# An FNet mixer gated with a SwiGLU block on one core: the opening loads, the first operand splits and the place of TensorE's flag read

## The chip, the core and the metric

The kernel runs on one core of a Trainium2 chip. A core has five engines that run their own instruction queues: TensorE (PE, matrix products, with its weight loads shown apart as PEld), VectorE (DVE), ScalarE (ACT), GpSimd (POOL) and SyncE (SP, which here only issues DMAs). The metric is the device time of one execution in microseconds (us). The kernel before took 355.21 us, the median of three runs (354.94 to 356.22).

## What is computed

The input `x` is 2048 x 512 in float32. Branch A is the real part of a two-dimensional Fourier transform, written with given cosine and sine matrices. Branch B is a SwiGLU block with 1376 hidden columns. A gate per row mixes the two:

```
g = sigmoid((x * gate_w).sum(-1, keepdims=True))
a = x @ dft_hid_re.T ; b = x @ dft_hid_im.T
A = dft_seq_re @ a - dft_seq_im @ b
B = (silu(x @ w1) * (x @ w3)) @ w2
out = g * A + (1 - g) * B
```

## The kernel before, in words

All products are of float32 values. Each operand is split into a rounded high part (a type that TensorE reads fast) and the low rest, and a product is three matmuls, high x high, high x low and low x high (`mm3`, line 131). The high part is a copy on ScalarE (`high`, line 114) or, for half of a tile, on VectorE (`high_by_both`, line 463, whose VectorE half is line 465); the low part is a subtraction on VectorE that reads the high part (`low`, line 117). Weights and `x` are cut into blocks and combined so that seven block products do the work of eight; these are the tiles `X`, `Y` and `Z`. The first group of them, written out by hand, accumulates in four banks `C`.

The program has three stretches. Up to about 207 us it forms the gate and up products of branch B (tiles `C`, `X`, `Y`, `Z`), 16 matmul groups of 128 x 512 per weight block, while VectorE and ScalarE split the next operands and sum products. Then come 528 matmuls of the down product (tile `H`). The end, from 321 us on, is the Fourier branch (tiles `O`, `E`, `Y`, `Yodd`) with the output stores. The Fourier branch uses symmetries of the cosine and sine matrices. That they hold is tested while the kernel runs; one value, the flag, says whether they do (lines 581 to 593). Every engine loads it into a register (lines 1328, 1342 and 1373) and then branches: with the symmetries there, the branch leaves out a general path (line 1380).

The order of instructions is the order of the Python code, engine by engine; nothing is rescheduled. The opening stands in lines 413 to 534. The array `first` packs, for each of 128 partitions, the first weight block and the blocks `B11` and `B21` of `x`: columns 0 to 255 are the first quarter of the weights (`W0[0]`), 256 to 1279 are `B11` in two halves of 512, 1280 to 1535 are another quarter, and so on to 3071. SyncE loads it in four pieces of 768 columns (lines 416 and 417), then two more blocks of `x` (`xs_B`, line 174) and the weight blocks 1 to 5 (`ws`, line 198). While the first piece is on its way, TensorE runs nine matmuls on constants (line 423, tile `wps`). Then lines 474 to 486 split the pieces as they come; the splits land in `xo` (`x`), `wa` (weights) and `a` (the quarter at 1280), and `half` (line 435) issues six matmuls each. For the first one the order of operands is: high weights x high `x`, high weights x low `x`, low weights x high `x`, for the first half of `x`, then high x high, low x high, high x low for the second.

After the opening, VectorE's queue holds without a pause: the splits of `B12` and `B22` (lines 490 to 493), the block differences (line 181), the splits of the next weight blocks and, from line 364 on, the sums of each item (`gate_up`). TensorE meets the results of that queue by semaphores.

Of the kernel before, what the change touches and what calls it, by code (L numbers as in the profile page):

```python
# [18 lines left out]
NTB = S // TB  # L19
NC = (F + P - 1) // P  # L20
NP2 = (NC + 1) // 2
WARM = 9
LOOK = 3
K = 9
TOL = 2.0 ** 40
# [5 lines left out]
def fnet_swiglu_gate_kernel(  # L31
# [27 lines left out]
    nc = tc.nc  # L59
# [26 lines left out]
    def bank(k, name):  # L86
        return psum.tile([P, 512], F32, tag=f"ps{k}", name=name)
# [20 lines left out]
    def free(*tiles):  # L108
        for t in tiles:
            _, places, at = HELD.pop(id(t))  # L110
            if places is not F4 or at not in GONE:
                places.append(at)

    def high(hi, src):
        nc.scalar.activation(hi, src, AF.Copy)  # L115

    def low(hi, lo, src):
        nc.vector.tensor_sub(lo, src, hi.bitcast(F32))  # L118

    def split(hi, lo, src):  # L120
        high(hi, src)
        low(hi, lo, src)
# [20 lines left out]
    def flat(ap):  # L143
        return ap.rearrange("p a n -> p (a n)")
# [268 lines left out]
    ctx.enter_context(tc.manual_schedule())  # L413
    XO[0] = xo0.tile([P, 2, 7, 2, 512], F32R, tag="xo", name="xo0")
    raw = xo1.tile([P, 2, 6, 2, 512], F32, tag="xo", name="raw")[:, 0].rearrange("p i q n -> p (i q n)")
    for n in range(4):
        nc.sync.dma_start(raw[:, 768 * n : 768 * n + 768], first[:, 768 * n : 768 * n + 768])
    ST[0, "B11"], ST[0, "B21"] = raw[:, 256:1280], raw[:, 1792:2816]
    W0 = [raw[:, at : at + 256] for at in (0, 1536, 2816, 1280)]
    warm = nc.const_aps.tensor(1.0, [P, 512], mybir.dt.bfloat16)  # L420
    wps = bank(7, "wps")
    for n in range(WARM):
        nc.tensor.matmul(wps, warm[:, :P], warm, start=True, stop=True)
# [11 lines left out]
    def half(i, j, w, x, start):  # L435

        wp = lambda h, sl: a21[:, h, sl] if w is None else WA[0][:, h, w, sl]
        xp = lambda q, h: b12[:, h, q * 512 : (q + 1) * 512] if x is None else XO[0][:, h, x, q, :]  # L440
        hh, lh, hl = (0, 0), (1, 0), (0, 1)
        order = [(r, *p) for r in range(2)
                 for p in ((hh, lh, hl) if x is None or r and w == x else (hh, hl, lh))]
        for n, (r, u, v) in enumerate(order):
            matmul(C[i, j], wp(u, slice(r * P, (r + 1) * P)), xp(r, v),
                   start=start and n == 0, stop=not start and n == 5)

    def xo_half(k, q):
        i = OPS.index(k)
        return XO[0][:, 0, i, q], XO[0][:, 1, i, q], ST[0, k][:, q * 512 : (q + 1) * 512]  # L450
# [12 lines left out]
    def high_by_both(hi, lo, src):  # L463
        high(hi[:, :256], src[:, :256])
        nc.vector.tensor_copy(hi[:, 256:], src[:, 256:])

    def split_by_both(hi, lo, src):
        high_by_both(hi, lo, src)
        low(hi, lo, src)

    def w0_parts(w):
        return flat(WA[0][:, 0, w : w + 1]), flat(WA[0][:, 1, w : w + 1]), W0[w]

    high_by_both(*xo_half("B11", 0))
    high(*w0_parts(0)[::2])
    low(*xo_half("B11", 0))
    low(*w0_parts(0))
    split(*xo_half("B11", 1))
    half(0, 0, 0, 0, True)
    split(a21[:, 0], a21[:, 1], W0[3])  # L480
    half(1, 0, None, 0, True)
# [91 lines left out]
    n = NI - 1 - LOOK  # L573
# [7 lines left out]
    def verdict():  # L581


        v = acc.rearrange("p (g n) -> p g n", n=16)
        nc.vector.scalar_tensor_tensor(v, v, TOL, rep_sum[:, :5, None].to_broadcast([P, 5, 16]),
                                       op0=ALU.mult, op1=ALU.is_le)
        nc.vector.tensor_reduce(flag[:, :1], acc, axis=mybir.AxisListType.X, op=ALU.add)

    def sum_flags(ps):
        nc.tensor.matmul(ps[:1, :1], flag[:, :1], nc.const_aps.tensor(1.0, [P, 1], F32), start=True, stop=True)  # L590

    def see_flags(ps):
        nc.vector.tensor_scalar(flag[:1, 2:3], ps[:1, :1], 80.0 * P, None, op0=ALU.is_lt)
# [40 lines left out]
    def work(eng, us, most=9, lag=None, over=0.3):  # L634


        NOW[0] += 1
        TOKENS[0] = min(TOKENS[0] + RATE[0], 1.5)
        lag = LAG[0] if lag is None else lag
        for i in ORDER[:LIMIT[0]]:  # L640
            of, cost, f, after, _, _, temps = QUEUE[i]
            if i in ISSUED or of != eng:
                continue
            if most == 0 or us < cost - over:
                break
            if i not in LOADED or NOW[0] - LOADED[i] < lag or temps and len(F4) < temps + RES[0]:
                continue
            if any(NOW[0] - ISSUED.get(k, NOW[0]) < (GAP.get(i, 1) if lag else 1) for k in after):
                continue
            HELD_BACK[0] -= temps  # L650
            f()
            ISSUED[i] = NOW[0]
            us -= cost
            most -= 1
        load_ahead(AHEAD[0])
        return us
# [561 lines left out]
    def next_two(name):  # L1218
        turn[0] += 1
        return psum.tile([P, 1024], F32, tag=f"two{(3, 1, 2, 0)[turn[0] % 4]}", name=name)  # L1220
# [76 lines left out]
    def of_d(im, odd):  # L1297
        at = 514 * im + 258 * odd
        return [DT[:, h, at : at + 258 - 2 * odd].rearrange("p (a n) -> p n a", a=2) for h in range(2)]

    def chain_two(to, terms):
        for n, (u, v) in enumerate(terms):
            for k, (i, j) in enumerate(((0, 0), (0, 1), (1, 0))):
                nc.tensor.matmul(to, u[i], v[j], start=n == k == 0, stop=n == len(terms) - 1 and k == 2,  # L1304
                                 skip_group_check=True)
# [3 lines left out]
    bad_in, seen = nc.alloc_registers("bad"), flag.bitcast(I32)[0:1, 2:3]  # L1309
    z_E = yp.tile([P, 2, 2, 516], F32R, tag="z_E2", name="z_E2")  # L1310

    def even(p):
        two = next_two(f"E2_{p}")
        ps = two[:, :258], two[:, 512:770]
        forms(*ps, ("E2",), range(2), p)
        z = Z["E2", p] = z_E[:, p]
        zh, zl = (z[:, h].rearrange("p (v n) -> p v n", v=2) for h in range(2))
        split(zh, zl, two.rearrange("p (v n) -> p v n", v=2)[:, :, :258])

    even(0)  # L1320
    for u, (kind, za, zb, n, swap) in enumerate(UNITS):
        if u == 4:
            even(1)
        ps = next_two(f"Y{u}")
        if u == 5:
            sum_flags(ps)
        if u == 8:
            nc.tensor.reg_load(bad_in[mybir.EngineType.PE], seen)

        def zs(p, at):  # L1330
            return [Z[kind, p][:, h, at : at + P] for h in range(2)]

        apart = u == len(UNITS) - 1
        po = next_two("Yodd") if apart else ps
        evens, odds = (v[:, lo:hi].rearrange("p (n a) -> p n a", a=2)
                       for v, lo, hi in ((ps, 254, 512), (po, 512, 768)))
        chain_two(evens, [(zs(0, za), of_d(0, 0)), (zs(1, zb), of_d(1, 0))])
        chain_two(odds, [(zs(1, za), of_d(0, 1)), (zs(0, zb), of_d(1, 1))])
        if u == 5:
            see_flags(ps)  # L1340
            for e in (nc.sync, nc.gpsimd, nc.scalar):
                e.reg_load(bad_in[e.engine], seen)
        r = yp.tile([P, 1024], F32, tag=f"r{u % 6}", name=f"r{u}")
        nb = NB.pop(u)

        def both(v):
            return v.rearrange("p (a m) -> p a m", a=2)[:, :, :256]

        for i in range(0 if apart else n):
            k = FIRST[u] + i  # L1350
            rv, nv = (both(v[:, i * D : i * D + D]) for v in (r, nb))
            src = both(ps[:, 255:769])[:, :, ::-1] if i ^ swap else both(ps[:, 254:770])
            nc.vector.scalar_tensor_tensor(rv, src, g_pos[:, k : k + 1], nv, op0=ALU.mult, op1=ALU.add)
        if apart:
            k = FIRST[u]
            for a, src in enumerate((ps[:, 255:511], po[:, 512:768])):
                at = slice(256 * a, 256 * a + 256)
                nc.vector.scalar_tensor_tensor(r[:, at], src[:, ::-1], g_pos[:, k : k + 1], nb[:, at],  # L1358
                                               op0=ALU.mult, op1=ALU.add)
                nc.sync.dma_start(out[k][:, at], r[:, at])  # L1360
            continue
        nc.sync.dma_start(out[FIRST[u] : FIRST[u] + n].rearrange("k p n -> p k n"),
                          r.rearrange("p (k n) -> p k n", k=2)[:, :n])
        if FIRST[u] > 7:
            free(nb)
        if u < 2:
            work("A", 3.6)
            work("D", 1.3)
        if u == 2:
            work_until(set(range(n_late)))  # L1370
        if u == 3:
            verdict()
    nc.vector.reg_load(bad_in[mybir.EngineType.DVE], seen)
    bad = nc.snap(bad_in, donate=True, min_val=0, max_val=0x3F800000)
    close(zo_a_cm, lp_cm)
# [255 lines left out]
```

## Time and profile before

| what | value |
|---|---|
| median of three runs | 355.21 us (354.94 to 356.22) |
| the profiled execution's own time | 355.75 us |
| its span, first to last instruction | 354.0 us |
| TensorE busy | 348.0 us, 98% of the span |
| VectorE, ScalarE, GpSimd busy | 311.2, 233.5, 73.3 us |
| moved by DMA | 103.03 MB, 291 GB/s in the mean |

A profile's times are counted from the first instruction of the span. A row of the timeline holds the start, the time from the first to the last of the merged instructions, the engine, the line of the kernel, the operation, output tile <- input tiles, shapes and the count; in brackets stands the idle time of that engine just before, and what ended it. Matmuls overlap, so six of them that start 0.216 us apart and take 0.379 us each stand as one row of 1.46 us.

### The profile page before, as it was taken

The numbers are of one execution on the slowest core, as the hardware profiler recorded it, in microseconds if no ns is written. First come the engines' busy times: TensorE is split into PE (matmuls) and PEld (weight loads), VectorE is DVE, ScalarE is ACT, GpSimd is POOL, SyncE is SP. The second block draws the span as 40 slices with busy tenths as digits, with TensorE's granted clock in tenths as the row PEclk, the third lists the DMA queues.
The fourth block names the chain that finished last, engine by engine and source line by source line (L and its number), as shares of the span: only waits on it lengthen the run. The fifth ranks groups of instructions, "written<-read, shape, count | busy, mean of one in ns | idle before, by whom it ended". The sixth has DMA issues, their size and how long they took to land.

```text
span 354.0 us, 5152 instructions
## 1 busy us (share of the span) xinstructions
PE 348.0 (98%) x1718; PEld 303.7 (86%) x1718; DVE 311.2 (88%) x442; ACT 233.5 (66%) x395; POOL 73.3 (21%) x121
## 2 busy tenths in 40 slices
PE   8999999999999999999999999999999999999994
PEld 4888888888888888888888888888888888889994
DVE  4999989999869788888887899989969989998983
ACT  5875866556648687775433399642588988879940
POOL 0012333323111132111113763335011002000000
PEclk9999999999999999999999999999999999999999
DMA  7669865669645779999999149997649999999276
GB/s 279 254 244 357 319 261 212 224 240 332 222 120 192 250 218 390 408 400 402 373 382 291 58 126 373 410 365 241 237 120 362 416 411 406 411 409 348 100 262 219
DMA packets 33952, 103.03 MB, mean 291 GB/s; under 512 B 5874, under 2 KB 6276, under 8 KB 33924
## 3 DMA queue, kind: packets, MB, share of 16 engines
q1 hardware_dynamic: 26340, 75.91, 58.2%
q0 software_dynamic: 7584, 26.77, 20.6%
q8 instruction: 14, 0.23, 0.3%
q14 instruction: 14, 0.11, 0.1%
HBM read 78.02 MB, written 24.65 MB: 290 GB/s over the span
## 4 chain that ended last, share of the span: by engine, by line
PE 96%; DMA 1%; ACT 1%; DVE 0%; issue 0%; SPq 0%; ACTq 0%
PE H L129 32%; PE X L129 30%; PE Z L129 15%; PE Y L129 8%; PE Y L1304 4%; PE C L129 3%; PE O L129 3%; PE E L129 1%; DMA raw<-first 1%; PE Yodd L1304 0%; DVE h L408 0%; ACT w2t L115 0%; ACT u L369 0%; DVE r L1358 0%; ACT xo L115 0%
## 5 line engine op out<-in xcount | busy, mean ns | idle before, releaser
L129 PE MATMUL H<-w2t,ht 128*128 128x512 f32 (+1 forms) x528 | 114.1, 379 | 0.0
L129 PEld LDWEIGHTS H<-w2t,ht 128*128 128x128 f32 (+1 forms) x528 | 99.8, 189 | 14.2
L129 PE MATMUL X<-xo,wb 128*128 128x512 f32 x378 | 88.6, 379 | 0.0
L129 PEld LDWEIGHTS X<-xo,wb 128*128 128x128 f32 x378 | 71.4, 189 | 10.2
L765 ACT ACTIVATE t<-t 128x1024 f32<-128x1024 f32 (+1 forms) x68 | 67.3, 992 | 1.5 <-DVE t L754 1.4
L320 POOL DMA_DIRECT2D hs<-h x36 | 19.6, 545 | 88.7 <-DVE h L391 63.5
L404 ACT ACTIVATE h<-X 128x512 f32<-128x512 f32 x21 | 12.5, 596 | 32.2 <-PE X L129 21.8
L129 PE MATMUL Z<-xo,wa 128*128 128x512 f32 x126 | 30.7, 380 | 0.0
L129 PE MATMUL X<-xo,wa 128*128 128x512 f32 x126 | 30.8, 380 | 0.0
L115 ACT ACTIVATE ht<-hr 128x1024 fp32r<-128x1024 f32 x19 | 20.0, 1053 | 16.3 <-PE H L129 10.6
L129 PE MATMUL Y<-xo,wa 128*128 128x512 f32 x126 | 30.6, 379 | 0.0
L129 PE MATMUL Z<-xo,wb 128*128 128x512 f32 x126 | 30.6, 379 | 0.0
L381 DVE TENSOR_TENSOR u<-u,X 128x512 f32<-128x512 f32 x21 | 14.4, 686 | 17.9 <-PE X L129 13.4
L129 PEld LDWEIGHTS Z<-xo,wa 128*128 128x128 f32 x126 | 23.7, 189 | 3.8 <-ACT u L369 0.4
L129 PEld LDWEIGHTS X<-xo,wa 128*128 128x128 f32 x126 | 23.7, 189 | 3.6 <-DVE wa L118 0.3
L129 PEld LDWEIGHTS Y<-xo,wa 128*128 128x128 f32 x126 | 23.8, 189 | 3.4
L129 PEld LDWEIGHTS Z<-xo,wb 128*128 128x128 f32 x126 | 23.8, 189 | 3.4
L754 DVE TENSOR_TENSOR t<-t,rep 128x1024 f32<-128x1024 f32 x21 | 24.7, 1220 | 0.6 <-DMA t<-wt 0.6
L118 DVE TENSOR_TENSOR ht<-hr,ht 128x1024 fp32r<-128x1024 f32 x19 | 23.1, 1217 | 0.0
L115 ACT ACTIVATE wa<-ws 128x768 fp32r<-128x768 f32 x19 | 15.9, 838 | 6.2 <-PE Z L129 5.9
L752 DVE TENSOR_TENSOR t<-t,rep 128x512 f32<-128x512 f32 x30 | 19.0, 684 | 0.0
L756 DVE TENSOR_TENSOR t<-t,rep 128x1024 f32<-128x1024 f32 x16 | 18.7, 1220 | 0.0
(210 smaller groups left out, 519.6 us busy)
## 6 DMA issues: line engine op xcount, KB each, us to landing
t<-wt SPq DMA_DIRECT2D x60, 512.0 KB, 9.3
hr<-hs SPq DMA_DIRECT2D x19, 512.0 KB, 8.8
hs<-h POOLq DMA_DIRECT2D x36, 256.0 KB, 4.4
wbsp<-wb POOLq DMA_DIRECT2D x16, 512.0 KB, 4.8
wb<-wbsp SPq DMA_DIRECT2D x16, 512.0 KB, 9.4
xr<-xw SPq DMA_DIRECT2D x8, 512.0 KB, 11.6
xs_B<-xt SPq DMA_DIRECT2D x6, 512.0 KB, 6.5
ws<-w POOLq DMA_DIRECT2D x6, 512.0 KB, 4.0
```

What stands on the lines that cost most here:

```text
L115: nc.scalar.activation(hi, src, AF.Copy)
L118: nc.vector.tensor_sub(lo, src, hi.bitcast(F32))
L129: nc.tensor.matmul(ps.rearrange("p (n a) -> p n a", a=2), u, turns(v)[:, some], **kw)
L320: nc.gpsimd.dma_start(hs[c][:, b * TB : (b + 1) * TB], h)
L381: nc.vector.tensor_add(u4, u4, x)
L404: nc.scalar.activation(g1, x, AF.Silu)
L752: f(*(v[:, 512 * a : 512 * a + 512] for v in (t, t, r)))
L754: nc.vector.tensor_sub(t, t, r)
L756: nc.vector.tensor_add(t, t, r)
L765: nc.scalar.activation(t[:, :n], t[:, :n], AF.Abs, accum_out=acc[:, i : i + 1])
L1304: nc.tensor.matmul(to, u[i], v[j], start=n == k == 0, stop=n == len(terms) - 1 and k == 2, skip_group_check=True)
```

## The change

It has three parts. First, `WARM` goes from 9 to 8, so one matmul on constants fewer runs at the start. Second, the array `first` is loaded in five pieces: columns 0 to 255 by GpSimd, then 256 to 767 (the first half of `B11`), 768 to 1535, 1536 to 2303 and 2304 to 3071 by SyncE. The splits behind it change order: the weights' high and low parts come first, then the first half of `B11`, with its high part done by both engines as before, and the second half of `B11` is now split by both engines too, where ScalarE copied its whole high part. Third, TensorE's load of the flag leaves its place ahead of the ninth unit of the Fourier branch and stands behind all its products, written twice.

```diff
-WARM = 9
+WARM = 8
...
-    for n in range(4):
-        nc.sync.dma_start(raw[:, 768 * n : 768 * n + 768], first[:, 768 * n : 768 * n + 768])
+    for n, (lo, hi) in enumerate(((0, 256), (256, 768), (768, 1536), (1536, 2304), (2304, 3072))):
+        (nc.sync if n else nc.gpsimd).dma_start(raw[:, lo:hi], first[:, lo:hi])
...
-    high_by_both(*xo_half("B11", 0))
-    high(*w0_parts(0)[::2])
-    low(*xo_half("B11", 0))
-    low(*w0_parts(0))
-    split(*xo_half("B11", 1))
+    split(*w0_parts(0))
+    split_by_both(*xo_half("B11", 0))
+    split_by_both(*xo_half("B11", 1))
...
-        if u == 8:
-            nc.tensor.reg_load(bad_in[mybir.EngineType.PE], seen)
...
+    for _ in range(2):
+        nc.tensor.reg_load(bad_in[mybir.EngineType.PE], seen)
     nc.vector.reg_load(bad_in[mybir.EngineType.DVE], seen)
```

This is VectorE's queue at the start of the program, as a difference: minus was there before, plus is there now. `wa` is the split of the first weights, `xo` that of `x`, `raw` the loaded array, `a` another quarter of the weights; `DMAHW0` is SyncE's first load, `DMASW0` GpSimd's.

```order
+L118 TENSOR_TENSOR wa_135<-raw,wa_135 128x256 [waits DMASW0_49,Activation_49]
 L465 CAST xo_100<-raw 128x256 [waits DMAHW0_49]
 L118 TENSOR_TENSOR xo_100<-raw,xo_100 128x512 [waits DVE_49,Activation_49]
-L118 TENSOR_TENSOR wa_135<-raw,wa_135 128x256 [waits Activation_49]
-L118 TENSOR_TENSOR xo_100<-raw,xo_100 128x512 [waits DMAHW1_49,Activation_49]
+L465 CAST xo_100<-raw 128x256 [waits DMAHW1_49]
+L118 TENSOR_TENSOR xo_100<-raw,xo_100 128x512 [waits DVE_49,Activation_49]
 L118 TENSOR_TENSOR a_128<-raw,a_128 128x256 [waits Activation_49]
 L465 CAST xo_100<-raw 128x256 [waits DMAHW2_49]
```

The weights' subtraction now stands at the head of VectorE's queue and waits for GpSimd's load and ScalarE's copy; a copy of a quarter of `B11` is new.

This is the end of TensorE's queue before; `Y` and `Yodd` are the last banks, `dt` and `z_E` operands of the Fourier branch, `tail` holds the flag.

```order
L1304 MATMUL Y_3326<-dt,z_E_3149 128x256 x6
L1328 TENSOR_LOAD tail [waits DVE_49]
L1304 MATMUL Y_3342<-dt,z_E_3149 128x258 [waits DVE_49,PE_49]
L1304 MATMUL Y_3342<-dt,z_E_3149 128x258 x5
L1304 MATMUL Y_3342<-dt,z_E_3149 128x256 x6
L1304 MATMUL Y_3359<-dt,z_E_3149 128x258 [waits DVE_49,PE_49]
L1304 MATMUL Y_3359<-dt,z_E_3149 128x258 x5
L1304 MATMUL Yodd<-dt,z_E_3149 128x256 [waits DVE_49]
L1304 MATMUL Yodd<-dt,z_E_3149 128x256 x5
L1380 COMPARE_AND_BRANCH
```

And this is the same end now (line numbers are those of the changed file, two lower).

```order
L1302 MATMUL Y_3343<-dt,z_E_3150 128x258 [waits DVE_49,PE_49]
L1302 MATMUL Y_3343<-dt,z_E_3150 128x258 x5
L1302 MATMUL Y_3343<-dt,z_E_3150 128x256 x6
L1302 MATMUL Y_3359<-dt,z_E_3150 128x258 [waits DVE_49,PE_49]
L1302 MATMUL Y_3359<-dt,z_E_3150 128x258 x5
L1302 MATMUL Yodd<-dt,z_E_3150 128x256 [waits DVE_49]
L1302 MATMUL Yodd<-dt,z_E_3150 128x256 x5
L1370 TENSOR_LOAD tail [waits DVE_49]
L1378 COMPARE_AND_BRANCH
```

The load stands behind the last product now, and it stands there once: of the two that are written, the built program keeps one, with the wait for VectorE ahead of it.

## The prediction, made before the changed kernel was run

> **What bounds the kernel now.** I read the page's shares first, then the chain that ended last.
>
> ```profile
> PE 348.0 (98%) x1718; PEld 303.7 (86%) x1718; DVE 311.2 (88%) x442; ACT 233.5 (66%) x395; POOL 73.3 (21%) x121
> PE 96%; DMA 1%; ACT 1%; DVE 0%; issue 0%; SPq 0%; ACTq 0%
> ```
>
> TensorE is busy 98% of the span and carries 96% of the chain, so only the waits left in its queue can be won. The view of waits, for its weight loads, names them.
>
> ```profile
> PEld C L129 <- ACT wa L115: 1.2, 1, 1.2
> PEld C L129 <- DVE xo L118: 0.5, 2, 0.3
> ...
> PEld X L129 <- DVE wa L118: 0.3, 1, 0.3
> ```
>
> The change touches the first two. Whether a gain there survives depends on the last row, a wait for VectorE. The timeline of the opening:
>
> ```profile
> 0.84 1.81 SPq L417 DMA_DIRECT2D raw<-first  x4
> 0.91 4.01 PE L423 MATMUL wps<-const-bfloat16-1.0 128*128 128x512 bf16 x9 [0.91 <-PEq L1618]
> ...
> 4.40 0.42 ACT L115 ACTIVATE xo<-raw 128x256 fp32r<-128x256 f32 x1 [2.16 <-DMA raw<-first]
> 4.40 0.29 DVE L465 CAST xo<-raw 128x256 fp32r<-128x256 f32 x1 [4.40 <-DMA raw<-first]
> 4.72 0.40 ACT L115 ACTIVATE wa<-raw 128x256 fp32r<-128x256 f32 x1
> 4.85 0.69 DVE L118 TENSOR_TENSOR xo<-raw,xo 128x512 fp32r<-128x512 f32 x1 [0.15 <-ACT xo L115]
> ...
> 5.17 2.06 PE L129 MATMUL C<-xo,wa 128*128 128x512 f32 x6 [0.25 <-ACT wa L115]
> 5.34 0.64 ACT L115 ACTIVATE xo<-raw 128x512 fp32r<-128x512 f32 x1 [0.22 <-DMA raw<-first]
> 5.46 0.42 DVE L118 TENSOR_TENSOR wa<-raw,wa 128x256 fp32r<-128x256 f32 x1
> ...
> 6.01 0.69 DVE L118 TENSOR_TENSOR xo<-raw,xo 128x512 fp32r<-128x512 f32 x1
> 6.57 0.42 ACT L115 ACTIVATE xo<-raw 128x256 fp32r<-128x256 f32 x1 [0.29 <-DMA raw<-first]
> ...
> 7.93 0.42 ACT L115 ACTIVATE xo<-raw 128x256 fp32r<-128x256 f32 x1 [0.63 <-DMA raw<-first]
> ...
> 8.68 0.69 DVE L118 TENSOR_TENSOR xo<-raw,xo 128x512 fp32r<-128x512 f32 x1
> 9.17 1.15 ACT L115 ACTIVATE b<-xs_B 128x512 fp32r<-128x512 f32 x2 [0.52 <-DMA xs_B<-xt]
> ...
> 9.43 1.38 PEld L129 LDWEIGHTS C<-xo,wa 128*128 128x128 f32 x7 [0.22 <-DVE xo L118]
> ...
> 10.45 1.06 ACT L115 ACTIVATE xo<-xs_B 128x1024 fp32r<-128x1024 f32 x1
> ...
> 11.54 1.23 DVE L118 TENSOR_TENSOR xo<-xs_B,xo 128x1024 fp32r<-128x1024 f32 x1 [0.41 <-ACT xo L115]
> ```
>
> The four pieces reach ScalarE at 4.40, 5.34, 6.57 and 7.93. TensorE begins at 5.17, once the weights' copy (second on ScalarE) is there, and waits again at 9.43 for a subtraction of the last piece. Two rows later VectorE is idle for 0.41 until ScalarE has copied a block that two later loads bring: 10.45 is 0.13 behind the end of the copies before it (9.17 + 1.15), so a landing released it. From there VectorE starts anew, whatever the opening did. How far that start reaches is seen in the busy times of a stretch (us, then PE, PEld, DVE, ACT, POOL with counts) and in the timeline around 36 us.
>
> ```profile
> 11.54:31.98 20.44, 20.44 (x96) 17.89 (x95) 19.98 (x28) 14.60 (x23) 1.35 (x3) 1.00 0.69 256
> ```
>
> ```profile
> 34.35 1.46 PE L129 MATMUL Z<-xo,wb 128*128 128x512 f32 x6
> 35.11 0.95 DVE L118 TENSOR_TENSOR wa<-ws,wa 128x768 fp32r<-128x768 f32 x1
> 35.65 1.60 PE L129 MATMUL X<-xo,wa 128*128 128x512 f32 x6
> ...
> 36.12 0.73 PEld L129 LDWEIGHTS X<-xo,wa 128*128 128x128 f32 x4 [0.28 <-DVE wa L118]
> ```
>
> VectorE is busy 19.98 of 20.44 us. So from 11.54 on it is a queue of work without slack, and its subtraction that ends at 35.11 + 0.95 = 36.06 holds TensorE at 36.12. The six matmuls at 35.65 take 1.60 where six undisturbed ones take 1.46, so TensorE loses 0.14 there. TensorE's time at 36 is the later of its own and VectorE's.
>
> **The change part by part.** *The loads.* Let w be the landing of GpSimd's 128 KB. ScalarE's copy (0.40) and VectorE's subtraction (0.42, the next instruction starts some 0.33 after its start) now stand ahead of the copies of `x`. VectorE's copy of `x` therefore starts no earlier than w + 0.40 + 0.03 + 0.33 = w + 0.76; its end 0.29 later releases the first matmul, and the subtraction of `x` follows (0.69). Then comes the added copy for the second half (0.29, next 0.33 after), and its subtraction. With w = 4.0: copy 4.76, first matmul 5.10, subtractions at 5.09 and 6.03, against 6.01 before. So w = 4.0 is the break-even: the subtraction that left (next one 0.55 after its start) pays for the added copy and the wait. An earlier w advances the opening by as much, down to about 0.3: the last piece lands at 7.93 as before, its copy takes 0.42, and its subtraction (8.40 + 0.69) then releases TensorE at 9.13, not 9.43. A later w delays all of it by as much, since VectorE's queue up to 9.4 has no gap to absorb it.
>
> When does w fall? No load by GpSimd stands in the opening. The nearest rows: loads of weights by it from 46 to 85 us, its smallest load from memory on busy queues, and its first DMA of the program.
>
> ```profile
> DMA to landing us min/median/max: 3.2/3.5/5.1
> ```
>
> ```profile
> spc<-misc POOLq DMA_DIRECT2D x1, 16.0 KB, 3.1
> ...
> wbsp<-wb POOLq DMA_DIRECT2D x1, 512.0 KB, 5.1
> ```
>
> The first row is for five loads of 384 or 512 KB, the second for 16 KB, the third a store. 128 KB lies between the first two, so I take 3.2 behind an issue at about 0.85, where SyncE's first stands: w = 4.05. The bounds are 3.45 (256 KB less than the least of those loads, 0.6 at the 418 GB/s shown below) and 5.95 (as slow as the first store). The Trainium skill (page "DMA: Bandwidth & Descriptors", section "Anatomy of one DMA — SWDGE (gpsimd) path") fits such a transfer with about 2.0 us plus its bytes over 436 GB/s. That would be 2.3 us here, an estimate, and w near 3.1, so the full 0.3 at the opening; no run here shows a GpSimd load that fast.
>
> *What becomes of it.* VectorE's start at 11.54 hangs on a landing, not on the opening: up to 0.41 of lateness on VectorE is absorbed, and no earliness is passed on. A gain of 0.3 on TensorE therefore ends at 36.12, where it waits 0.3 longer for the same subtraction: 0.0. A loss up to 0.14 is absorbed at the same place; a greater one goes through less 0.14. The landing itself can move: the bytes are the same, but a piece of 3 KB a partition is now one of 1 KB and one of 2 KB.
>
> ```profile
> 6.00:7.00 1.00, 1.00 (x5) 0.66 (x5) 0.99 (x3) 0.71 (x3) 0.00 (x0) 1.00 0.93 376
> 10.00:11.00 1.00, 1.00 (x6) 0.89 (x5) 1.00 (x2) 0.88 (x2) 0.00 (x0) 1.00 1.03 418
> ```
>
> The last number is GB/s: rows of 3 KB move at 376, rows of 4 KB at 418, a tenth less. Another tenth for 384 KB (1.0 us at 376 GB/s) is 0.1 later; a second queue that fills the start earlier could give 0.1 to 0.3 back: no row shows that, and SyncE's pieces need some 1 us each in any case. I take +0.1, from the rate, with bounds -0.3 and +0.2.
>
> *The warm-up matmul.* Nine start (4.01 - 0.63) / 8 = 0.42 apart, so one less ends at 4.5 instead of 4.92. With the first product at 5.1 nothing waits for it: 0.0, if TensorE's speed does not hang on it (a rival below).
>
> *The flag.*
>
> ```profile
> L1328 PEldq TENSOR_LOAD <-tail x1: 1064/1064/1064, 344.4 to 344.4; - x1
> ```
>
> ```profile
> 332.70 5.52 PE L1304 MATMUL Y<-dt,z_O 128*128 128x258 f32 x48
> 343.72 4.85 PE L1304 MATMUL Y<-dt,z_E 128*128 128x258 f32 x42
> ```
>
> ```profile
> L1380 PEldq COMPARE_BRANCH x1: 397/397/397, 347.1 to 347.1; - x1
> L1380 PEldq EVENT_SEMAPHORE x1: 51/51/51, 349.3 to 349.3; - x1
> ```
>
> ```profile
> L1624 SPq EVENT_SEMAPHORE x14: 17/28/28, 351.4 to 353.9; - x14
> ```
>
> The load takes 1.06 in TensorE's sequencer, which runs ahead: with it, 42 matmuls start (4.85 - 0.275) / 41 = 0.112 apart; without it, 48 start (5.52 - 0.275) / 47 = 0.112 apart. Its removal gives 0.0. At the new place it starts about where the branch starts now, 347.1; 1.06 and 0.40 behind it make 348.6, still ahead of 349.3, where the sequencer waits for the last products anyway. SyncE ends the program at 351 to 354 by waiting for stores. A second load, were it kept, would end at 349.7, with over 1 us to spare: 0.0 either way. That the program keeps one read of the two is thus a part of the change that isn't done, at no price.
>
> *The sum.* Opening +0.05, gone at 36.12; landing +0.1; warm-up 0.0; flag 0.0: about +0.1 on the profiled execution's 354.0 of span and 355.75 of its own time. That execution lies 0.54 above the median of the runs shown, so the sum is put on the median: 355.21 + 0.1 = 355.3.
>
> **The rivals.** *The gain stays.* The first bytes come by two queues, the block behind 10.45 lands 0.3 sooner, and VectorE's whole queue moves with TensorE. For it: two queues can fill the first microseconds sooner than one. Against it: the bytes are the same, and small rows move slower. 355.21 - 0.3 = 354.9.
>
> *GpSimd's load is late* (the slower one). It decides from w = 4.0 + 0.14 on, at VectorE's head, where everything else is queued behind the weights' subtraction. For it: the first DMA of GpSimd took 5.1. Against it: that one moved four times the bytes. With w = 5.95 the loss is 1.95 - 0.14 = 1.8, and the time 357.0.
>
> *TensorE stays slow longer.*
>
> ```profile
> L423 PE MATMUL wps<-const-bfloat16-1.0 x9: 601/634/634, 0.9 to 4.3; 128*128 128x512 bf16 x9
> L129 PE MATMUL C<-xo,wa x30: 379/379/652, 5.2 to 16.0; 128*128 128x512 f32 x30
> ```
>
> Matmuls of 512 columns take 634 ns up to about 5.2, the first product 652, later ones 379: TensorE changes speed right at the first products, some 4.5 us after its first matmul. If the idle stretch ahead of them, 0.3 longer at worst, puts that off by 3.4 us to about 9, matmuls 0.42 apart until then make about 9.5 where now 15 are done: 5.5 x 0.216 = 1.2, less 0.14 and 0.1 of waits that vanish, +1.0, 356.2. That stretch of 3.4 us is what the Trainium skill gives for its clock gate (page "TensorE: Matmul & The Clock Gate", section "What's actually happening"): a free-running window of 3.4 us has to be busy. The rows agree in that the speed changes once, early; no run here shows how busy is enough. By the rows alone, the change of speed took 4.5 us of matmuls with a gap of 0.25 in them, so such a gap does no harm.
>
> **How the numbers follow.** A measurement of this kernel can tell about 0.5%, 1.8 us, from no change. Chances: nothing left of it 62% (355.3, by the landing's bounds 355.0 to 355.5), the gain stays 20% (354.9), slow longer 9% (356.2), late load 9% (up to 357.0, half of it beyond 1.8). The runs before scatter by 0.3 below and 1.0 above their median. The range goes from 354.9 - 0.3 = 354.6 to 356.2 and leaves out the late load and some scatter. Slower by over 0.5%: 0.05; faster by as much would take six times the best gain worked out: 0.01; the rest, 0.94, is no change.
>
> **What would show it.** In the changed kernel's timeline: ScalarE's first copy of `wa` gives w (about 4.05); the weight loads at 9.43 come between 9.1 and 9.5; VectorE's start at 11.54 moves by 0.1 at most; the wait of `X` for `wa` near 36.12 grows by what the opening won, and TensorE's first matmul behind it stays within 0.1; matmuls near the end stay 0.112 apart, with one load of the flag about 347. A wait at 36.12 that moves forward with the opening, a w beyond 4.3, or 634 ns matmuls beyond 6 us would make it wrong.

## The result, and the profile after

The changed kernel takes 359.81 us in the median (359.31 to 359.82), the kernel before 355.26 in the runs beside it: a ratio of 1.0119, with a 95% interval from 1.0093 to 1.0145. It is slower by 1.2%, where no change was forecast. One run of the changed kernel (752.41) and one of an experiment below, warm_19 (411.31, whose profile is of that run), lie far from all others and are left out of the ranges and ratios; why they were so long is not settled.

The profiled execution took 359.81 us, its span 357.9, so 3.9 more than before. The page of the changed kernel, with the busy times and the chain that ended last:

```profile
PE 348.9 (97%) x1717; PEld 304.8 (85%) x1717; DVE 312.0 (87%) x443; ACT 233.1 (65%) x395; POOL 70.1 (20%) x122
PE 95%; DVE 2%; DMA 1%; issue 1%; ACT 0%; DVEq 0%; ACTq 0%; POOLq 0%
```

TensorE is busy for 0.9 us more, though it has one matmul fewer: some ran slower. The other 3 us are waits. The opening, in the timeline:

```profile
0.91 3.59 PE L423 MATMUL wps<-const-bfloat16-1.0 128*128 128x512 bf16 x8 [0.91 <-PEq L1616]
1.28 0.75 POOL L417 DMA_DIRECT2D raw<-first  x1 [0.85 <-POOLq L1616]
...
6.18 0.42 ACT L115 ACTIVATE wa<-raw 128x256 fp32r<-128x256 f32 x1 [3.94 <-DMA raw<-first]
...
6.63 0.42 DVE L118 TENSOR_TENSOR wa<-raw,wa 128x256 fp32r<-128x256 f32 x1 [6.63 <-ACT wa L115]
6.97 0.29 DVE L465 CAST xo<-raw 128x256 fp32r<-128x256 f32 x1
...
7.40 0.45 PE L129 MATMUL C<-xo,wa 128*128 128x512 f32 x1 [2.90 <-DVE xo L465]
...
8.11 2.20 PE L129 MATMUL C<-xo,wa 128*128 128x512 f32 x5 [0.25 <-DVE xo L118]
...
9.28 1.15 ACT L115 ACTIVATE b<-xs_B 128x512 fp32r<-128x512 f32 x2 [0.54 <-DMA xs_B<-xt]
...
10.10 2.33 PE L129 MATMUL C<-xo,a 128*128 128x512 f32 x6
...
10.57 1.06 ACT L115 ACTIVATE xo<-xs_B 128x1024 fp32r<-128x1024 f32 x1
```

GpSimd's load is issued at 1.28; by the chain of waits it lands 4.87 later, and ScalarE starts on it at 6.18. VectorE, whose queue is headed by the subtraction of these weights, does nothing until 6.63. The first product comes at 7.40; before it was 5.17. The bracket on that row is the second thing to read: TensorE idled 2.90 ahead of it, since the eight warm-up matmuls end at 4.50. Then it runs slowly: six matmuls take 2.33 at 10.10, and six took 1.46 before. The windows of the changed kernel (length, then busy time and count of PE, PEld, DVE, ACT, POOL, then the granted clock, the busy share of the DMA engines and GB/s) show when:

```profile
1.60:5.04 3.44, 2.90 (x7) 0.76 (x5) 0.00 (x0) 0.63 (x2) 0.43 (x1) 1.00 0.87 275
5.04:8.45 3.41, 0.80 (x3) 0.50 (x4) 1.61 (x5) 2.27 (x8) 0.00 (x0) 1.00 1.03 382
8.45:11.86 3.41, 3.41 (x10) 2.65 (x9) 3.20 (x8) 2.50 (x4) 0.00 (x0) 0.50 1.02 418
```

and this is the third of these windows in the kernel before:

```profile
8.45:11.86 3.41, 3.41 (x17) 2.84 (x16) 2.78 (x6) 2.77 (x5) 0.00 (x0) 1.00 1.02 414
```

In the same 3.41 us TensorE does 10 matmuls at a clock of 0.50 and did 17 at 1.00. The full clock was there ahead of that, from 5.04 to 8.45, while TensorE had only 0.80 us of work. (The 1.00 of the first row, up to 5.04, is no full speed: its seven matmuls in 2.90 us are 0.42 apart. The column stays at 1.00 until the trace holds a first change.) How the lateness goes on is seen from the same rows in both kernels. Before:

```profile
11.04 1.46 PE L129 MATMUL C<-b,wa 128*128 128x512 f32 x6
...
204.36 1.16 PEld L129 LDWEIGHTS Z<-xo,wa 128*128 128x128 f32 x6 [0.45 <-ACT u L369]
...
348.41 0.83 PE L1304 MATMUL Yodd<-dt,z_E 128*128 128x256 f32 x6
```

And in the changed kernel, with the wait at the end of the opening and the place where the rest of the time goes:

```profile
14.86 1.46 PE L129 MATMUL C<-b,wa 128*128 128x512 f32 x6
...
22.90 0.69 DVE L290 TENSOR_TENSOR s<-s,Y 128x512 f32<-128x512 f32 x1 [1.77 <-PE Y L129]
...
38.91 0.95 DVE L118 TENSOR_TENSOR wa<-ws,wa 128x768 fp32r<-128x768 f32 x1
...
39.92 0.73 PEld L129 LDWEIGHTS X<-xo,wa 128*128 128x128 f32 x4 [0.26 <-DVE wa L118]
...
201.95 1.26 POOL L966 TENSOR_TENSOR row<-row 1x512 f32<-1x512 f32 x1 [2.81 <-DMA row<-edges]
202.35 3.11 DVE L828 TENSOR_TENSOR t<-t,dh 128x516 f32<-128x516 f32 x2
...
208.63 0.51 PEld L129 LDWEIGHTS Z<-xo,wa 128*128 128x128 f32 x3 [0.93 <-ACT u L369]
...
352.69 0.83 PE L1302 MATMUL Yodd<-dt,z_E 128*128 128x256 f32 x6
```

So TensorE is 2.23 late at its first product (7.40 against 5.17), 3.82 at its 25th (14.86 against 11.04, with the full clock back), 3.80 at the wait for `wa` (39.92 against 36.12) and 4.27 at the wait near 208 (208.63 against 204.36). VectorE does not make up for it: at 22.90 it has itself waited 1.77 for a product of TensorE, where it had not waited before. The last products start 4.28 later (352.69 against 348.41), and the end takes 0.4 less: 3.9. The late load is the 2.23, the slow clock the 1.6 that follow: seven products fewer in its window, 0.216 each, are 1.5. The 0.47 near 208 come with two subtractions on VectorE that take 3.11 instead of 2.64 while GpSimd works on rows beside them. That is only observed, and their length alone does not set the wait: in sync_warm_10, below, they take 2.92, and TensorE waits 0.23 there.

### The profile page after: what moved, and what is told of

It reads as the page before. It is cut to its first block, busy times and chain, and to the rows that moved or that the text cites. A ratio compares the mean times of both kernels' runs of the same rounds, so it can differ in the third digit from the quotient of the medians.

```text
span 357.9 us, 5155 instructions
## 1 busy us (share of the span) xinstructions
PE 348.9 (97%) x1717; PEld 304.8 (85%) x1717; DVE 312.0 (87%) x443; ACT 233.1 (65%) x395; POOL 70.1 (20%) x122
## 4 chain that ended last, share of the span: by engine, by line
PE 95%; DVE 2%; DMA 1%; issue 1%; ACT 0%; DVEq 0%; ACTq 0%; POOLq 0%
PE H L129 32%; PE X L129 29%; PE Z L129 15%; PE Y L129 8%; PE Y L1302 4%; PE C L129 3%; PE O L129 3%; DMA raw<-first 1%; PE E L129 1%; DVE t L828 1%; DVE xo L118 0%; DVE h L408 0%; PE Yodd L1302 0%; DVE h L390 0%; ACT u L369 0%
## 5 line engine op out<-in xcount | busy, mean ns | idle before, releaser
L129 PEld LDWEIGHTS X<-xo,wb 128*128 128x128 f32 x378 | 71.4, 189 | 10.2
```

The lines of the kernel that those rows point to most:

```text
L129: nc.tensor.matmul(ps.rearrange("p (n a) -> p n a", a=2), u, turns(v)[:, some], **kw)
```

## The experiments

Each group ran beside the kernel before on the same chip: 355.36 us in the median for the first group (quarter_by_sync to warm_19), 355.71 for the second (idle_gpsimd_loads to sync_warm_10), 355.65 for the third. The theory after the result: the load by GpSimd lands late and TensorE idles for it (2.2 us), and that idle stretch drops its clock (1.6 us). The rivals: the new order of the splits, the shorter warm-up by itself, the flag.

**quarter_by_sync**: the changed kernel without GpSimd.

```diff
-        (nc.sync if n else nc.gpsimd).dma_start(raw[:, lo:hi], first[:, lo:hi])
+        nc.sync.dma_start(raw[:, lo:hi], first[:, lo:hi])
```

> The changed kernel with one thing put back: all five pieces of the first load are issued by SyncE, the quarter of the weights first. Theory (GpSimd's load is late, and the idle stretch it makes on TensorE lets the clock fall back): the quarter lands before 4.0, the first product starts at 4.9 to 5.3, the clock rises once, and the time is that of the kernel before, 355.3 within 0.5. Rival (the new order of the splits and the added copy cost the time): most of the loss stays, 357 or more.

Measured: 356.56 (355.63 to 358.6), a ratio of 1.0037 [1.002, 1.0053]. With GpSimd's load gone, 3.3 of the 4.5 us are gone. The median misses both forecasts: it lies 0.8 above the theory's range and 0.4 below the rival's. The timeline of the profiled execution, at 358.14 one of the longer of the eleven:

```profile
3.00 0.42 ACT L115 ACTIVATE wa<-raw 128x256 fp32r<-128x256 f32 x1 [0.76 <-DMA raw<-first]
...
4.60 1.95 PE L129 MATMUL C<-xo,wa 128*128 128x512 f32 x3
...
6.84 1.65 PE L129 MATMUL C<-xo,wa 128*128 128x512 f32 x3 [0.29 <-ACT xo L115]
...
8.28 2.19 PE L129 MATMUL C<-xo,a 128*128 128x512 f32 x5
```

The same quarter is there at 3.00, and the first product, at 4.60, is 0.57 earlier than before. Yet the kernel is not faster: here the slow clock lasts to 10.2 (five matmuls take 2.19 at 8.28), and TensorE waits for pieces between its first groups; that these waits keep the clock low is argued. Part of the loss thus stays without GpSimd.

**only_warm_8** and **only_flag_at_end**: one part of the change alone, in the kernel before.

```diff
-WARM = 9
+WARM = 8
```

> The kernel before with 8 warm-up matmuls in place of 9 and nothing else. Theory: one warm-up matmul less leaves 0.4 us more idle time ahead of the first product and costs nothing, 355.3 within 0.4. Rival (the shorter warm-up is what lets the clock fall back): some 6 to 10 products run at 0.427 us, 356.2 to 356.9.

Measured: 356.03 (355.42 to 357.36), 1.0025 [1.0012, 1.0039]. One matmul on constants less costs something: the median lies between the two forecasts, 0.3 above the theory's range and 0.2 below the rival's. It does so in part of the runs: seven of twelve lie at 355.42 to 356.09, four at 357.00 to 357.36. The profiled one took 355.59 and shows the full clock from its first products on, so the long ones were not seen from inside.

The other one puts the flag's two loads behind the products, and nothing else:

```diff
-        if u == 8:
-            nc.tensor.reg_load(bad_in[mybir.EngineType.PE], seen)
...
+    for _ in range(2):
+        nc.tensor.reg_load(bad_in[mybir.EngineType.PE], seen)
```

> The kernel before with TensorE's load of the flag behind its last products and nothing else. Theory: 355.3 within 0.4, matmuls near the end 0.112 us apart as before. Rival (the load at the end is paid in full, or its removal ahead of the ninth unit frees something): slower by 1.06, or faster by up to that.

Measured: 355.97 (355.16 to 357.38), 1.0012 [0.9999, 1.0024]: not told from no change, nor from a loss of up to 0.24%; the median lies 0.3 above the theory's range. The views of the line and of the branch behind it, in the changed kernel:

```profile
L1370 PEldq TENSOR_LOAD <-tail x1: 909/909/909, 351.5 to 351.5; - x1
```

```profile
L1378 PEldq COMPARE_BRANCH x1: 393/393/393, 352.5 to 352.5; - x1
L1378 PEldq EVENT_SEMAPHORE x1: 51/51/51, 353.6 to 353.6; - x1
```

```profile
336.98 5.52 PE L1302 MATMUL Y<-dt,z_O 128*128 128x258 f32 x48
...
348.00 4.85 PE L1302 MATMUL Y<-dt,z_E 128*128 128x258 f32 x42
```

One load of 0.91 and a branch end at 352.9, and the sequencer waits at 353.6 for the products anyway. The 42 matmuls that had the load among them before take 4.85, as they did.

**warm_19**: the changed kernel, late load and all, with the idle stretch filled.

```diff
-WARM = 8
+WARM = 19
```

> The changed kernel with 19 warm-up matmuls, so that TensorE is busy until about 7.0 us. Theory (two costs: the late load 2.2 us, the clock's return to half speed 1.6 us): the first product still starts at about 7.4, but none behind it is 0.427 us apart, and the time is 359.8 - 1.6 = 358.2. Rival (the clock is no cost of its own, VectorE's late queue sets all): 359.8 stays.

Measured: 357.37 (357.21 to 357.92), 1.0055 [1.0039, 1.0071]. What is left is the late load, 357.37 - 355.36 = 2.0, near the 2.2 of the theory. What went, 359.81 - 357.37 = 2.4, hung on the idle stretch; the theory had said 1.6, and 358.2 for the time. The stretch is filled in the profiled execution, the one named above as left out:

```profile
7.20 0.46 PE L129 MATMUL C<-xo,wa 128*128 128x512 f32 x1 [0.17 <-DVE xo L465]
```

TensorE idles 0.17 ahead of its first product instead of 2.90. The granted clock there is 0.85, so this trace does not show the speed of the other runs.

**idle_gpsimd_loads**: is GpSimd's load slow by itself? Two loads that nobody reads, in the kernel before:

```diff
+    for n in range(2):
+        nc.gpsimd.dma_start(raw[:, 3072 + 256 * n : 3328 + 256 * n], first[:, 256 * n : 256 * n + 256])
```

> The kernel before, with two more loads of 128 x 256 from the array first, by GpSimd at the head of its queue, into columns that nothing reads. Theory (the first load by GpSimd is slow by itself): with all four of SyncE's pieces as before, the first of the two lands 4.6 to 5.1 us behind its issue, first packet 2.5 us or more behind it; the second, issued right behind, lands within 0.6 us of the first. Rival (only the order of the change's loads made it late, since SyncE's bytes go first): the first lands within 3.5 us. Both: nobody waits for the two, so the first product stays within 5.0 to 5.6 and the time within 0.6 us of the kernel before, but xs_B may land up to 0.6 later for the 256 KB more (0.6 = 256 KB at 418 GB/s).

Measured: 356.04 in one run. The view of this line says:

```profile
DMA to landing us min/median/max: 4.6/5.0/5.5
```

The first took 4.6 as the theory said, the second 5.5 from an issue 0.75 later, so it landed 1.6 behind the first and not within 0.6. That SyncE's bytes were on the way in this kernel too left the question open; gpsimd_alone, below, answers it against the theory.

**weights_second**: the changed kernel's loads with the splits in the order of before.

```diff
-    split(*w0_parts(0))
-    split_by_both(*xo_half("B11", 0))
-    split_by_both(*xo_half("B11", 1))
+    high_by_both(*xo_half("B11", 0))
+    high(*w0_parts(0)[::2])
+    low(*xo_half("B11", 0))
+    low(*w0_parts(0))
+    split(*xo_half("B11", 1))
```

> The changed kernel (GpSimd's quarter, 8 warm-up matmuls, the flag behind the products), with the order of the splits as in the kernel before: the first half of x ahead of the weights on VectorE and ScalarE. Theory (the late load itself costs, and the order adds one subtraction and one copy between the landing and the first product): the landing stays at 6.1 +- 0.3, the copy of wa follows it, the first product comes at 6.6 +- 0.3 instead of 7.40, and the time falls by 0.7 to 359.1 if the clock of TensorE still falls back, to 357 where it does not. Rival (only the landing counts, since VectorE's queue is full behind it): within 0.3 of the changed kernel, 359.5 to 360.1.

Measured: 357.28 (356.37 to 359.69), 1.0062 [1.0036, 1.0087]. The order counts, against the rival, but the theory's numbers miss too: it had the landing at 6.1 and, with the clock falling back, 359.1. The timeline:

```profile
3.65 0.42 ACT L115 ACTIVATE xo<-raw 128x256 fp32r<-128x256 f32 x1 [1.41 <-DMA raw<-first]
...
5.45 0.42 ACT L115 ACTIVATE wa<-raw 128x256 fp32r<-128x256 f32 x1 [1.39 <-DMA raw<-first]
...
5.92 2.93 PE L129 MATMUL C<-xo,wa 128*128 128x512 f32 x6 [1.42 <-ACT wa L115]
```

With `x` split while the weights are still on their way, the first product follows their copy by 0.47 (5.45 to 5.92); in the changed kernel it is 1.22 (6.18 to 7.40). The landing came 0.7 earlier than the same loads gave in the changed kernel, which the theory had not said, and the two add up to a first product 1.48 earlier. The clock is slow here too: the first six products take 2.93. But its price is 1.2 instead of 1.6 (the 25th product comes at 13.03, 1.99 late, and 0.75 of that is the first product's), and the wait near 206 is 0.17 instead of 0.93. These four make up the 2.5 between the two spans; only 0.75 of it is the order's alone.

**quarter_by_act**: the changed kernel with the quarter loaded by ScalarE's queue.

```diff
-        (nc.sync if n else nc.gpsimd).dma_start(raw[:, lo:hi], first[:, lo:hi])
+        (nc.sync if n else nc.scalar).dma_start(raw[:, lo:hi], first[:, lo:hi])
```

> The changed kernel with the first quarter of the weights loaded by ScalarE's queue instead of GpSimd's; all else the same. Theory (it is GpSimd's queue that is slow, not a second queue): the quarter lands at 3.0 to 3.6, xs_B as in the kernel before (SyncE again issues four pieces, not five), first product at 4.4 to 4.8; time 355.0 to 356.0, below the 356.56 of the quarter by SyncE, if its fifth issue caused part of the 1.2 us that stayed there. Rival (what stayed there is TensorE's clock alone, after 8 warm-up matmuls and waits between the first products): again 356.5 +- 0.4, with single runs above 357.5. Second rival (any second queue disturbs the first pieces): the quarter lands beyond 5, time above 357.5.

Measured: 356.29 (355.56 to 357.75), 1.0018 [1.0004, 1.0032]; the median lies 0.3 above the upper end that the theory gave, and one run goes beyond 357.5, as the rival said. Its timeline:

```profile
3.33 0.42 ACT L115 ACTIVATE wa<-raw 128x256 fp32r<-128x256 f32 x1 [0.68 <-DMA raw<-first]
...
4.56 0.45 PE L129 MATMUL C<-xo,wa 128*128 128x512 f32 x1 [0.18 <-DVE xo L465]
...
36.33 0.73 PEld L129 LDWEIGHTS X<-xo,wa 128*128 128x128 f32 x4 [0.57 <-DVE wa L118]
```

A second queue alone does not make the quarter late, against the second rival. And here the opening gains what the change may have been meant to gain, 0.6 at the first product, with the clock full from there on in the profiled execution. It ends where the prediction said: the wait for `wa` near 36 has grown from 0.28 to 0.57, and TensorE leaves it at 36.33, 0.2 later than before.

**sync_warm_10** and **act_warm_10**: the quarter by SyncE, and by ScalarE, each with 10 warm-up matmuls.

```diff
-WARM = 8
+WARM = 10
```

> The changed kernel with the quarter loaded by SyncE, and 10 warm-up matmuls instead of 8. They end at about 5.3 at the slow clock, so the first product comes at 5.3 instead of 4.60 and the waits behind it (0.44, 0.29 and more) shrink. Theory (the clock falls back where TensorE idles before and between its first products): no run above 357.2, median 355.3 to 356.0. Rival (the fifth load of SyncE, which puts xs_B 0.45 us later, and the order of the splits): median stays 356.3 to 356.9.

Measured: 356.05 (355.7 to 357.62), 1.0017 [1.0006, 1.0029], against 1.0037 with eight. One run passes 357.2, and the median lies just above the theory's range; the step is in its direction, but the two intervals overlap.

> The quarter by ScalarE's queue, with 10 warm-up matmuls instead of 8: no fifth load on SyncE, no late quarter, no idle stretch ahead of the first product. Theory (what stays of the loss without GpSimd's load is the clock): within 0.3 of the kernel before. Rival (the order of the splits itself costs, by the added copy on VectorE): 0.5 to 0.8 above it. If the earlier first product were worth something, it would be 0.3 or more below; the queue of VectorE up to the wait near 36 us says that it isn't.

Measured: 356.38 (355.13 to 356.84), 1.0014 [1.0001, 1.0027]: 0.5 by the ratio and 0.7 by the medians, which is the rival's range and not the theory's 0.3; nothing lies above 356.84. In this one the wait near 36 is:

```profile
36.13 0.73 PEld L129 LDWEIGHTS X<-xo,wa 128*128 128x128 f32 x4 [0.59 <-DVE wa L118]
```

First product 4.79 instead of 5.17, and 36.13 instead of 36.12 here: nothing is left of the gain. Why this kernel stays 0.1% above the kernel before isn't settled. The rival's cause, the added copy on VectorE, is not seen in the profiled execution: its last products start 0.1 earlier than before (348.30 against 348.41). What is longer is the end, 6.1 from there to the end of the span against 5.6. That end takes 5.2 to 6.2 in the seven kernels profiled with the flag's load behind the products (warm_19 aside) and 5.4 to 5.6 in the six with the load in its old place, so the moved load is as much a suspect for the 0.1 to 0.2% that stay; no run separates the two.

**before_warm_3** and **before_warm_11**: the kernel before with fewer and more matmuls on constants.

```diff
-WARM = 9
+WARM = 3
```

> The kernel before with 3 warm-up matmuls instead of 9 and nothing else: they end at 2.4, so TensorE idles about 2.8 ahead of its first product at 5.2, as long as in the changed kernel (2.9), while no load and no split is later. Theory (that idle stretch costs by itself, since the clock is then at half speed for one more window, and its price is the difference between the changed kernel, 359.81, and the same with 19 warm-up matmuls, 357.37): 1.6 to 2.5 over the kernel before, 357.2 to 358.1, with products 0.427 apart beyond 8. Rival (all of the change's loss is the late load, the clock is a side show): within 0.4 of the kernel before.

Measured: 357.61 (357.1 to 359.03), 1.0057 [1.0036, 1.0078]: 1.96 over the kernel before, for an idle stretch alone, with no load and no split moved. Its timeline, and its windows:

```profile
0.91 1.45 PE L423 MATMUL wps<-const-bfloat16-1.0 128*128 128x512 bf16 x3 [0.91 <-PEq L1618]
...
5.19 2.93 PE L129 MATMUL C<-xo,wa 128*128 128x512 f32 x6 [2.83 <-ACT wa L115]
```

```profile
4.36:7.77 3.41, 2.58 (x6) 2.10 (x7) 2.67 (x7) 2.57 (x7) 0.00 (x0) 1.00 1.02 396
7.77:11.18 3.41, 3.41 (x9) 2.69 (x9) 3.31 (x7) 2.74 (x5) 0.00 (x0) 1.00 1.03 419
11.18:14.60 3.42, 3.42 (x17) 2.99 (x17) 3.38 (x4) 2.29 (x5) 0.00 (x0) 1.00 0.91 367
```

Here the counts must be read, and not the clock column, which stays at 1.00 where the trace holds no change: 9 matmuls from 7.77 to 11.18 and 17 behind it. The first product stands at 5.19, as before, and the slow stretch lasts 6 us.

The same place in the kernel before, with two matmuls more:

```diff
-WARM = 9
+WARM = 11
```

> The kernel before with 11 warm-up matmuls. They end between 5.2 and 5.8, depending on when the clock rises, and leave no idle stretch ahead of the first product. Theory (the nine of the kernel before already cover the gap): median within 0.3 of the kernel before, and fewer runs beyond 356.2. Rival (two more matmuls stand in the way of the first product by up to 0.6, of which 0.14 is absorbed at 36 us): 0.3 to 0.5 slower. A median of 0.4 or more below the kernel before would say that its gap of 0.25 costs too, and would beat both kernels.

Measured: 355.86 (355.13 to 356.42), 1.0007 [0.9997, 1.0017]. Nine are enough, and none of the variants tried beats the kernel before. The theory's fewer runs beyond 356.2 did not come: four of twelve here, two of 23 in the kernel before.

**gpsimd_alone**: the same load with the DMA engines to itself, since SyncE's first piece now writes the same columns behind it and waits for its landing.

```diff
+    nc.gpsimd.dma_start(raw[:, 0:256], first[:, 0:256])
     for n in range(4):
```

> The kernel before, with GpSimd loading the first quarter (128 x 256) ahead of SyncE's four pieces, the first of which writes the same columns again and so waits for its landing: GpSimd's load has all DMA engines to itself. Theory (GpSimd's first DMA starts late by itself): first packet 2.4 us or more behind the issue at 1.28, landing 3.3 us or more behind it, so beyond 4.6. Rival (SyncE's pieces, issued first, hold the DMA engines): first packet within 1.4, landing within 2.2, before 3.5. Both: SyncE's loads start after the landing instead of at 0.84, so the time is 2.5 to 5 over the kernel before and says nothing by itself.

Measured: 360.32 in one run. The chain of waits and a window of this kernel:

```profile
1.28 2.54 DMA raw<-first
...
3.84 3.51 DMA raw<-first
```

```profile
2.00:3.84 1.84, 1.84 (x5) 0.60 (x4) 0.00 (x0) 0.23 (x2) 0.03 (x1) 1.00 0.21 71
```

and the windows of the changed kernel while it waits for the same load:

```profile
2.00:4.00 2.00, 2.00 (x6) 0.60 (x4) 0.00 (x0) 0.23 (x2) 0.03 (x1) 1.00 0.98 295
4.00:6.16 2.16, 0.50 (x2) 0.00 (x0) 0.00 (x0) 0.00 (x0) 0.00 (x0) 1.00 0.97 347
```

Alone, the load lands at 3.82, 2.54 behind its issue, with the DMA engines 0.21 busy. With SyncE's pieces, issued from 0.84 on, beside it, at a share of 0.97, it takes 4.87, and 4.6 and 4.1 in idle_gpsimd_loads and weights_second. The theory of a slow start on GpSimd's side falls: at 1.28 + 3.3 or later it should have landed beyond 4.6. The rival (SyncE's pieces hold the DMA engines) is nearer, though it landed 0.3 later than that said.

## Why the prediction was wrong

**What fails: the landing of GpSimd's load.** The prediction put "3.2 behind an issue at about 0.85, where SyncE's first stands: w = 4.05". The issue came at 1.28, 0.43 later, and the landing 4.87 behind it, 1.67 more than the row: w = 6.16, past the upper bound of 5.95 too. The row was for loads later in the program. The windows of the kernel before, at the opening and behind the first and the last of these five loads, say how they differ:

```profile
2.00:4.00 2.00, 2.00 (x6) 0.74 (x5) 0.00 (x0) 0.23 (x2) 0.00 (x0) 1.00 0.88 270
```

```profile
46.94:50.20 3.26, 3.26 (x17) 2.86 (x16) 2.48 (x4) 2.85 (x5) 1.26 (x3) 1.00 0.46 161
```

```profile
84.52:88.00 3.48, 3.48 (x17) 3.05 (x17) 3.44 (x7) 2.38 (x4) 1.98 (x4) 1.00 0.83 310
```

They met DMA engines that were 0.46 to 0.83 busy; the opening's were 0.88 busy in the kernel before, all of it with SyncE's bytes, and 0.97 in the changed kernel. The prediction sized the load by its bytes ("128 KB lies between the first two") and counted SyncE's pieces as "some 1 us each in any case"; it didn't ask what the one does to the other. How the engines share their time between the queues stays open. The estimate from the Trainium skill (page "DMA: Bandwidth & Descriptors", section "Anatomy of one DMA — SWDGE (gpsimd) path"), 2.3 us, is near the 2.54 of the load alone, so the figure was good for an empty queue, which the opening does not have.

**What holds: the chain behind w.** The sum gave VectorE's copy at w + 0.76 and the first product at w + 1.10, so 6.92 and 7.26 for 6.16; they came at 6.97 and 7.40. The price, w - 4.0 - 0.14 = 2.0, is the 2.0 that warm_19 measured, though its own landing in those runs was not seen. The rival of the late load had the mechanism and nearly the size (1.8), and a chance of 9%.

**What fails next: the rivals were priced one at a time.** A late load makes the idle stretch, and the idle stretch makes TensorE slow; the prediction gave each 9% and added them nowhere. Its stretch was "0.3 longer at worst"; it grew from 0.25 to 2.90. Its slow clock was a rise put off by 3.4 to about 9. In the changed kernel the clock rose at 5.04, with nothing to multiply, and fell at 8.45, behind the window with 0.80 us of work. And slow costs more than the 1.0 it gave: 1.6 in the trace of the changed kernel, 2.4 by the median of warm_19, and 1.96 alone in before_warm_3, where the slow part lasts to 11.18. In the traces late load and slow clock make 2.2 + 1.6 = 3.8 of the 3.9; by the medians they make 2.0 and 2.4. The 0.8 between the 1.6 and the 2.4 is not settled.

**The warm-up matmul**, 0.0, is wrong by a little: 0.25% [0.12, 0.39] by itself. "Such a gap does no harm" was read from one execution, in which it did none. That the gap of other executions falls badly in the clock's window fits with the two groups of times, but none of the long ones was profiled.

**Right**: the end of the gain. No gain in the opening gets past the wait for `wa` near 36 us, shown by two kernels whose first product came 0.6 and 0.4 earlier. The landing of `xs_B` came 0.11 and 0.12 later (9.28 and 10.57), forecast 0.1, which is luck: with the same loads weights_second has 8.69 instead of 9.28, and with the loads of before only_warm_8 has 8.69 instead of 9.17. The flag, as far as TensorE goes: matmuls 0.112 apart, load and branch done before the sequencer's wait. Its price of 0.0 lies within the interval of only_flag_at_end, but so does 0.24%, and the ends named under act_warm_10 leave that open.

## What to carry to other kernels

A DMA's duration is read from rows with the same queue ahead of it: look at the DMA share of the window in which it will run, and at who else has loads on the way, above all at the start of a program, where SyncE's queue alone kept the engines 0.88 busy from 2 us on. When a rival's mishap leaves TensorE idle, add what the idle time does to its clock to the same rival, since the two come together. And before an earlier start is counted as a gain, find the next place where the engine meets a queue without slack.

## What the runs showed of the hardware

- The same 128 KB load by GpSimd took 2.54 us alone and 4.1 to 4.9 with SyncE's pieces of 1.4 to 1.6 MB, issued from 0.84 on, beside it; by ScalarE's queue, issued at 0.73 ahead of SyncE's, its copy starts at 3.33.
- TensorE's clock went back to half after a window with 0.80 us of work in 3.41, for the next 3.41 us (0.50 from 8.45 to 11.86). The Trainium skill (page "TensorE: Matmul & The Clock Gate", section "What's actually happening") gives a window of 3413 ns and half speed behind an idle one; the trace agrees in the length (5.04, 8.45, 11.86), and the window ahead of the fall was not idle but held that 0.80. How busy is enough does not come out of the busy times: 2.90 us of 3.44 were (the window to 5.04 in the changed kernel), 2.58 of 3.41 were not (the one to 7.77 in before_warm_3), and neither were 3.09 of 3.42 in quarter_by_sync (3.36 to 6.78, if its windows end at 10.19, where the products go from 0.427 to 0.216 apart).
- The rise of the clock hits another place of the opening from one profiled execution to the next: the same eight warm-up matmuls take 3.40 us in only_warm_8, 3.46 in quarter_by_act and 3.59 in the changed kernel. Kernels with a longer gap there scatter more, 355.4 to 357.4 with 8 warm-up matmuls and 355.1 to 356.4 with 11; that the one makes the other is argued.
